# Turning the fourth tile of probabilities by DMA, scores in four banks, and a first head left unnormalized

## The chip, the core and the metric

The kernel runs on one core of one Trainium2 chip. A core has five engines that run their own instruction queues in order: TensorE (PE, with PEld for its weight loads), VectorE (DVE), ScalarE (ACT), GpSimd (POOL) and SyncE (SP), which here does nothing but issue DMAs. Matmuls write to PSUM, in banks of 128 partitions by 2 KB; the other tiles lie in SBUF. An engine waits for another through semaphores, and everything that stands behind a waiting instruction in the same queue waits with it.

The metric is the device time of one execution, in microseconds (us), as the median of several runs. Before the change it is 2786.77 us (three runs, 2785.22 to 2790.01 us).

## The reference

One block of a network: adaptive layer norm, attention over a window of cached keys and values, a second norm, and a gated MLP. Only the attention is touched by the change.

```python
W = min(4096, max(256, Sk // 4))          # 512 of 2048 cached positions
rep = Hq // Hkv                           # 32 query heads, 16 key heads
q = (x @ wq).reshape(B, Sq, Hq, Dh).transpose(0, 2, 1, 3)
k = jnp.repeat(k_cache[:, :, Sk - W:, :], rep, axis=1)
v = jnp.repeat(v_cache[:, :, Sk - W:, :], rep, axis=1)
scores = jnp.einsum("bhqd,bhkd->bhqk", q, k) * (Dh ** -0.5)
p = _softmax(scores, axis=-1)
o = jnp.einsum("bhqk,bhkd->bhqd", p, v)
return o.transpose(0, 2, 1, 3).reshape(B, Sq, Hq * Dh) @ wo
```

There are 2048 query rows of width 576, heads of 128, and an MLP of width 4608. Inputs and output are float32.

## The kernel before

Every float32 operand of a large matmul is split into two float16 tiles, a high part (the rounded value) and a low part (what is left). A product then takes three float16 matmuls: high by high, high by low, low by high.

**Slots.** The attention runs over 128 slots. A slot `i` is one query head on one block of 512 rows; the two heads that share a key head (`j` = 0 and 1) stand next to each other, so even slots are a first head and odd slots a second one. A slot has four steps, `t` = 0 to 3, one for each tile of 128 rows. The loop at the end of `tile_block` (L1465 to L1511) writes all queues by hand; the order of its calls is the order on each engine. Work of the MLP's preparation (splitting its weights, storing them) and the loading and splitting of the next heads' weights are hung in between by a table of tasks for each step (`run(i, t)`), and the last slots already begin the MLP.

**What happens to one tile.** `scores(i, t)` makes 128 by 512 scores with three matmuls in a PSUM bank (L400, from the pair of banks tagged "S"), and DVE takes their maximum (L404, L405, into one of three pairs of columns `nms`). `weights` takes the exponential on ACT (L417), which also sums the row into a column of `l`. The probabilities `p` must then be turned, because the value matmuls need the keys on the partitions. Tiles 0, 1 and 2 are split first, high by ACT (`half_high`, L449) and low by POOL (`half_low`, L454), into `hp`, and SP issues a DMA that turns both halves into `ptw` (`turn_away`, L461), two steps after the exponential's step. Tile 3 goes another way: at step 1 of the next slot PE turns the float32 tile with four transposes into a "T" bank (`turn`, L440), ACT copies the high part out of it (`turn_high`, L444), and at step 2 DVE subtracts for the low part (`turn_low`, L469).

**What happens to a slot.** At the end of slot `i`, after step 3, `values(i - 1)` runs its twelve matmuls of 512 columns (L479); each reads all four tiles of `ptw`. Queries of slot `i + 1` (L342, L346) are made in steps 0 to 2 of slot `i`, and each step holds one piece of the output projection of an older pair of heads (`back`, L353), two pieces of which fill the tile `E` (two banks, one buffer) that DVE then adds to `acc` (L507). The sums `l` are inverted on DVE (L424), stored as one row in DRAM (L427) and spread over all partitions as `r` by a second DMA (L430). At step 1 of slot `i + 2`, `normalize` multiplies the values by `r` on DVE (L488), and at step 3 `split_on` splits the result with ACT (L498) and POOL (L499) into the `o` that the projection reads.

**Buffers.** There are two "S" banks, two "T" banks, two "A" banks (queries and values take turns), four buffers of `p`, four of the tag `hf` (here `hp`), two of `ptw`.

## Time and profile before

| | before |
|---|---|
| median of three runs | 2786.77 us |
| lowest and highest | 2785.22 and 2790.01 us |
| the profiled execution | 2786.65 us |
| its span in the profile | 2784.8 us |
| granted TensorE clock | 0.996 |
| DMA packets, bytes | 594421, 463.27 MB |

The span runs from the first instruction of the program to the last; the profiled execution's own time is 1.85 us longer. "Busy" is the time in which an engine has an instruction in work; matmuls overlap, and their ends are modelled, so a PE that is shown busy can still have gaps. The chain in the page's fourth part is followed back from the last instruction to whatever released each step; PE has 50% of it, and the other engines and DMAs that it lists 6% together. In views that list a group, the numbers are its busy time in us, the mean duration of one instruction in ns, and behind the bar the idle time of the engine just before these instructions, with what ended it.

### The profile page before, as it was taken

How to read it: one execution, taken by the hardware profiler on the slowest of the kernel's cores; microseconds unless marked ns; L12 is line 12 of the kernel's file. 1: busy time of each engine (PE TensorE's matmuls, PEld its weight loads, DVE VectorE, ACT ScalarE, POOL GpSimd, SP SyncE). 2: the span in 40 equal slices, each digit the busy share in tenths (PEclk: the TensorE clock that was granted, in tenths of full speed). 3: DMA queues.
4: the chain of work that ended last, by engine and by line, in shares of the span. 5: the costliest groups of instructions: out<-in, count | busy, mean ns of one | idle time of the engine just before them, and what ended most of it. 6: DMA issues, size and time to landing. Idle time of an engine off the chain costs nothing.

```text
span 2784.8 us, 45011 instructions
## 1 busy us (share of the span) xinstructions
PE 2707.0 (97%) x15536; PEld 1535.3 (55%) x15536; DVE 2002.7 (72%) x3556; ACT 1624.1 (58%) x3022; POOL 1864.4 (67%) x1729
## 2 busy tenths in 40 slices
PE   6999999999999999999999999999999999999998
PEld 3455555555555555555555555555555555555555
DVE  7776788777788787887876657777766656566566
ACT  4686777777777877777677635544443333333332
POOL 3567788888788877777669637688774455333435
PEclk9999999999999999999999999999999999999999
DMA  5777888877777888878879945656643444333332
GB/s 162 177 168 187 189 186 185 179 178 187 169 181 172 187 200 186 212 181 205 194 185 220 233 125 169 195 165 199 206 152 103 160 123 127 104 102 112 105 110 77
DMA packets 594421, 463.27 MB, mean 166 GB/s; under 512 B 443152, under 2 KB 472976, under 8 KB 593424
## 3 DMA queue, kind: packets, MB, share of 16 engines
q1 hardware_dynamic: 593584, 460.39, 64.4%
q8 instruction: 122, 2.00, 0.3%
q14 instruction: 107, 0.88, 0.1%
q10 hardware_dynamic: 608, 0.00, 0.0%
HBM read 263.60 MB, written 95.99 MB: 129 GB/s over the span
## 4 chain that ended last, share of the span: by engine, by line
PE 50%; DVE 3%; DMA 1%; POOL 1%; issue 1%; ACT 0%; SPq 0%; DVEq 0%; POOLq 0%; ACTq 0%
PE py L764 15%; PE px L764 11%; PE pe L849 7%; PE pf L849 6%; PE pe L353 3%; PE po L479 2%; PE pss L400 2%; PE pq L342 2%; DMA row<-l 1%; DMA r<-row 0%; PE pt L440 0%; DVE acc L507 0%; DVE table L404 0%; PE pq L346 0%; POOL hp L454 0%
## 5 line engine op out<-in xcount | busy, mean ns | idle before, releaser
L454 POOL TENSOR_TENSOR hp<-p,hp 128x512 f16<-128x512 f32 x384 | 447.9, 1169 | 285.3 <-ACT hp L449 161.9
L417 ACT ACTIVATE p<-pss,table,factors 128x512 f32<-128x512 f32 x512 | 396.9, 775 | 362.0 <-DVE table L405 183.9
L764 PEld LDWEIGHTS <-wset 128*128 128x128 f16 x3528 | 345.7, 98 | 336.7 <-issue 4.0
L404 DVE TENSOR_REDUCE table<-pss 128x1 f32<-128x512 f32 x512 | 350.5, 685 | 211.8 <-PE pss L400 210.7
L764 PE MATMUL py<-hset,wset 128*128 128x512 f16 x2016 | 483.6, 380 | 0.0
L353 PE MATMUL pe<-o 128*128 128x288 f16 x3072 | 458.8, 286 | 14.6 <-DVE acc L507 12.5
L400 PE MATMUL pss<-k,qT 128*128 128x512 f16 x1536 | 417.3, 380 | 11.2 <-ACT p L417 9.2
L353 PEld LDWEIGHTS <-o 128*128 128x128 f16 x3072 | 300.4, 98 | 187.8 <-issue 20.9
L479 PE MATMUL po<-ptw,v 128*128 128x512 f16 x1536 | 358.2, 381 | 7.4 <-DVE ptw L469 5.6
L764 PE MATMUL px<-hset,wset 128*128 128x512 f16 x1512 | 361.5, 379 | 1.6 <-ACT p L417 1.6
L342 PE MATMUL pq<-hT,wq 128*128 128x512 f16 x1092 | 281.3, 380 | 1.1 <-DVE hT L211 1.1
L91 POOL TENSOR_TENSOR akv<-u,akv 128x512 f16<-128x512 f32 x141 | 164.8, 1178 | 174.6 <-ACT akv L90 166.8
L449 ACT CAST hp<-p 128x512 f16<-128x512 f32 x384 | 237.3, 618 | 12.9 <-POOL hT L213 0.4
L479 PEld LDWEIGHTS <-v 128*128 128x128 f16 x1536 | 150.9, 100 | 169.6 <-issue 16.8
L849 PEld LDWEIGHTS <-akv 128*128 128x128 f16 x1728 | 169.6, 98 | 93.6 <-issue 4.5
L400 PEld LDWEIGHTS <-qT 128*128 128x128 f16 x1536 | 150.4, 100 | 123.5 <-issue 12.6
L507 DVE SCALAR_TENSOR_TENSOR acc<-pe,factors,acc 128x576 f32<-128x576 f32 x256 | 207.7, 812 | 13.7 <-PE pe L353 10.4
L499 POOL TENSOR_TENSOR o<-on,o 128x512 f16<-128x512 f32 x128 | 150.2, 1173 | 55.8 <-ACT o L498 52.4
L342 PEld LDWEIGHTS <-wq 128*128 128x128 f16 x1104 | 108.6, 98 | 138.4 <-issue 9.0
L843 DVE SCALAR_TENSOR_TENSOR acc<-pf,table,acc 128x576 f32<-128x576 f32 x140 | 113.5, 811 | 80.6 <-PE pf L849 80.6
L944 ACT COPY u<-py 128x512 f32<-128x512 f32 x72 | 42.2, 586 | 200.5 <-PE py L764 198.6
L937 ACT ACTIVATE s<-s,table 128x512 f32<-128x512 f32 x72 | 52.0, 722 | 173.0 <-DVE s L936 173.0
(228 smaller groups left out, 4826.4 us busy)
## 6 DMA issues: line engine op xcount, KB each, us to landing
wset<-wd SPq DMA_DIRECT2D x213, 320.0 KB, 3.2
r<-row SPq DMA_DIRECT2D x128, 256.0 KB, 4.0
oset<-od SPq DMA_DIRECT2D x106, 288.0 KB, 3.2
wraw<-in_w SPq DMA_DIRECT2D x36, 768.0 KB, 5.5
wd<-wmade SPq DMA_DIRECT2D x75, 320.0 KB, 3.2
wset<-wd SPq DMA_DIRECT2D x71, 160.0 KB, 2.2
w2raw<-in_w SPq DMA_DIRECT2D x19, 576.0 KB, 4.9
wd<-ring SPq DMA_DIRECT2D x33, 320.0 KB, 2.8
```

What stands on the lines that cost most here:

```text
L91: eng.tensor_sub(halves[:, 1], src, halves[:, 0])
L342: nc.tensor.matmul(ps, w[:, k // 2, m, :], hT[:, DC + m if k == 1 else m, :], start=s == 0, stop=False)
L353: nc.tensor.matmul(E[:, h, :HALF], o[:, x, rows], w[:, y, h * HALF : (h + 1) * HALF], start=first and n == 0, stop=last and n == 2,)
L400: nc.tensor.matmul(pss, q[:, x, rows], k[:, y, :], start=n == 0, stop=n == 2)
L404: nc.vector.tensor_reduce(nm[:, 0:1], pss, axis=AX.X, op=ALU.max, negate=True)
L417: nc.scalar.activation(p, pss, AF.Exp, bias=nm[:, 1:2], scale=factor, accum_out=st["l"][:, t : t + 1])
L449: nc.scalar.copy(hp[:, 0, :], state[i]["p", t])
L454: nc.gpsimd.tensor_sub(hp[:, 1, :], state[i].pop(("p", t)), hp[:, 0, :])
L479: nc.tensor.matmul(po, v[:, x, c, :], pt[:, y, c, :], start=c == 0 and n == 0, stop=c == KC - 1 and n == 2)
L507: nc.vector.scalar_tensor_tensor(a, E[:, :, :HALF], factors[:, uses[u][0], 2:3], a, op0=ALU.mult, op1=ALU.add)
L764: nc.tensor.matmul(ps, w[:, a, :], h[:, b, :], start=start and n == 0, stop=stop and n == 6, skip_group_check=True)
L849: nc.tensor.matmul(ps[:, h, :HALF], a[:, rows], w[:, b, :], start=m == 0, stop=m == 2)
```

## The change

1. `turn`, `turn_high` and `turn_low` are gone. All four tiles go through `half_high`, `half_low` and `turn_away`. The fourth tile's `turn_away` stands at step 1 of the next slot, one step behind the third tile's.
2. Scores of tiles 0 and 2 go to the "T" banks that the transposes used, those of tiles 1 and 3 stay in "S".
3. The first head of a pair is no longer divided by its sums. `take_first` (ACT, step 0 of slot `i + 2`, one step before `normalize`) scales the values by 2^-24 straight from PSUM into the high part of `o`, and `normalize` makes the low part with one DVE instruction; its POOL subtraction, its row and its `r` are not made.
4. The second head is multiplied by the sum of the first over its own sum, so that both heads of a pair carry the same factor, one over the first head's sum. `E` is added to `acc` with that factor (a column of `l`) in place of a constant of the head. `l` is one tile for the pair, and DVE makes the ratio (a `scalar_tensor_tensor` on four columns) and the factor (a `tensor_scalar` on four columns) once a pair.

```diff
 def scores(i, t):
-        pss = bank("S", "pss")
+        pss = bank("S", "pss") if t % 2 else t_bank()
 def weights(i, t):
-            st["l"] = odd.tile([P, 2 * ST], F32, tag="l", name="l", bufs=3)
+            st["l"] = odd.tile([P, 6 * ST], F32, tag="l", name="l", bufs=4) if j == 0 else state[i - 1]["l"]
...
 def sums(i, step):
+        u, j, b = slots[i]
         st = state[i]
+        if j == 0:
+            return
+        first, both, up, ratio = (st["l"][:, lo * ST : hi * ST] for lo, hi in ((0, 1), (0, 2), (2, 4), (4, 5)))
         if step == 0:
-            nc.vector.reciprocal(st["l"][:, ST:], st["l"][:, :ST])
+            nc.vector.reciprocal(up, both)
+            nc.vector.scalar_tensor_tensor(ratio, first, O_DOWN, up[:, ST:], op0=ALU.mult, op1=ALU.mult)
         elif step == 1:
             st["row"] = dram.tile([P, ST], F32, name=f"row{i}")
-            nc.sync.dma_start(st["row"], st["l"][:, ST:])
+            nc.sync.dma_start(st["row"], ratio)
...
+    def take_first(i):
+        st = state[i]
+        o = st["o"] = new_o(i)
+        nc.scalar.activation(o[:, 0, :], st["po"], AF.Copy, scale=O_DOWN)
+
     def normalize(i):
         st = state[i]
         po = st.pop("po")
+        if slots[i][1] == 0:
+            o = st["o"]
+            nc.vector.scalar_tensor_tensor(o[:, 1, :], po, O_DOWN, o[:, 0, :], op0=ALU.mult, op1=ALU.subtract)
+            return
...
     def split_on(i):
         st = state[i]
+        if slots[i][1] == 0:
+            return
         on = st.pop("on")
-        o = st["o"] = pool.tile([P, 2, SB], F16, tag=("ah", "al")[i % 2], name="o", bufs=3)
+        nc.vector.tensor_scalar(
+            st["l"][:, 5 * ST :], st["l"][:, 2 * ST : 3 * ST], factors[:, uses[slots[i][0]][0], 2:3], 1.0 / O_DOWN,
+            op0=ALU.mult, op1=ALU.mult,
+        )
+        o = st["o"] = new_o(i)
...
 def attend_out(pair, t, j, total):
-                a, E[:, :, :HALF], factors[:, uses[u][0], 2:3], a, op0=ALU.mult, op1=ALU.add
+                a, E[:, :, :HALF], state[2 * pair]["l"][:, 5 * ST + t : 5 * ST + t + 1], a, op0=ALU.mult, op1=ALU.add
...
-            if t == 0 and 1 <= i <= n:
-                turn_away(i - 1, 2)
-            slot, tile = (i - 1 if t == 1 else n, ST - 1)
-            if 0 <= slot < n:
-                turn(slot, tile)
+            if t < 2 and 1 <= i <= n:
+                turn_away(i - 1, t + 2)
...
-            if 1 <= i <= n and t == 2:
-                turn_low(i - 1, ST - 1)
...
-            if t < 3 and i < n:
+            if i < n:
                 half_high(i, t)
                 half_low(i, t)
-            if t == 1 and 1 <= i <= n:
-                turn_high(i - 1, ST - 1)
+            if 2 <= i <= n + 1 and t == 0 and slots[i - 2][1] == 0:
+                take_first(i - 2)
```

How the queues move is shown at one place, slot 62 (a first head) and the beginning of slot 63. **SP**, from the first turning DMA of slot 62 on, before; `hp_9267`, `hp_9305` and `hp_9340` are its tiles 0 to 2, `hp_9407` is tile 0 of slot 63, `row61` and `row62` the sums of slots 61 and 62:

```order
L461 DMA_TRANSPOSE ptw_9329<-hp_9267 128x8x128
L636 DMA wd15_119<-wmade_9238 128x1280
L430 DMA r_9358<-row61_9309 128x512
L461 DMA_TRANSPOSE ptw_9329<-hp_9305 128x8x128
L461 DMA_TRANSPOSE ptw_9329<-hp_9340 128x8x128
L636 DMA wd15_119<-wmade_9323 128x640
L427 DMA row62_9447<-l_9264 128x4
L461 DMA_TRANSPOSE ptw_9464<-hp_9407 128x8x128
L636 DMA od70_168<-omade_9381 128x1152
L430 DMA r_9494<-row62_9447 128x512
```

The same place after; `hp_8901`, `hp_8937`, `hp_8970` and `hp_9000` are the four tiles of slot 62, `hp_9036` is tile 0 of slot 63:

```order
L455 DMA_TRANSPOSE ptw_8960<-hp_8901 128x8x128
L643 DMA wd15_119<-wmade_8872 128x1280
L436 DMA r_8988<-row61_8940 128x512
L455 DMA_TRANSPOSE ptw_8960<-hp_8937 128x8x128
L455 DMA_TRANSPOSE ptw_8960<-hp_8970 128x8x128
L643 DMA wd15_119<-wmade_8954 128x640
L455 DMA_TRANSPOSE ptw_8960<-hp_9000 128x8x128
L455 DMA_TRANSPOSE ptw_9085<-hp_9036 128x8x128
L643 DMA od70_168<-omade_9011 128x1152
```

The fourth tile's DMA has come in where the row of slot 62's sums stood, and that row and its `r` are gone.

**POOL**, from tile 0 of slot 62 to tile 0 of slot 63, before (`w2raw`, `wmade` and `omade` belong to the MLP's weights, `wq` to a later head):

```order
L454 TENSOR_TENSOR hp_9267<-p_9265,hp_9267 128x512
L275 TENSOR_TENSOR wq_9283<-wraw_8889,wq_9283 128x640
L735 TENSOR_TENSOR w2raw_8925<-w2raw_8925 128x288
L738 TENSOR_TENSOR w2raw_8925<-w2raw_8925 128x288
L454 TENSOR_TENSOR hp_9305<-p_9303,hp_9305 128x512
L686 TENSOR_TENSOR wmade_9323<-wraw_8707,wmade_9323 128x256
L687 TENSOR_TENSOR wmade_9323<-wraw_8707,wmade_9323 64x128
L454 TENSOR_TENSOR hp_9340<-p_9338,hp_9340 128x512
L499 TENSOR_TENSOR o_9370<-on_9301,o_9370 128x512
L718 TENSOR_TENSOR omade_9381<-w2raw_8925,omade_9381 128x2x288
L454 TENSOR_TENSOR hp_9407<-p_9405,hp_9407 128x512
```

And after:

```order
L448 TENSOR_TENSOR hp_8901<-p_8899,hp_8901 128x512
L276 TENSOR_TENSOR wq_8920<-wraw_8534,wq_8920 128x640
L742 TENSOR_TENSOR w2raw_8569<-w2raw_8569 128x288
L745 TENSOR_TENSOR w2raw_8569<-w2raw_8569 128x288
L448 TENSOR_TENSOR hp_8937<-p_8935,hp_8937 128x512
L693 TENSOR_TENSOR wmade_8954<-wraw_8368,wmade_8954 128x256
L694 TENSOR_TENSOR wmade_8954<-wraw_8368,wmade_8954 64x128
L448 TENSOR_TENSOR hp_8970<-p_8968,hp_8970 128x512
L448 TENSOR_TENSOR hp_9000<-p_8998,hp_9000 128x512
L725 TENSOR_TENSOR omade_9011<-w2raw_8569,omade_9011 128x2x288
L448 TENSOR_TENSOR hp_9036<-p_9034,hp_9036 128x512
```

In this even slot the low half of tile 3 takes the place of the subtraction of `o` (L499); in an odd slot both stand there.

**DVE**, steps 0 to 2 of slot 62 before (`table` holds the maxima):

```order
L404 TENSOR_REDUCE table<-pss 128x1
L405 TENSOR_SCALAR table<-table,factors 128x1
L424 RECIPROCAL l<-l 128x4
L404 TENSOR_REDUCE table<-pss 128x1
L405 TENSOR_SCALAR table<-table,factors 128x1
L488 TENSOR_TENSOR on<-po,r 128x512
L507 SCALAR_TENSOR_TENSOR acc_87<-pe,factors,acc_87 128x576
L404 TENSOR_REDUCE table<-pss 128x1
L405 TENSOR_SCALAR table<-table,factors 128x1
L469 TENSOR_TENSOR ptw<-pt,ptw 128x4x128
```

And after (`pt` is now a bank of scores):

```order
L405 TENSOR_REDUCE table<-pt 128x1
L406 TENSOR_SCALAR table<-table,factors 128x1
L429 RECIPROCAL l<-l 128x8
L430 SCALAR_TENSOR_TENSOR l<-l 128x4
L405 TENSOR_REDUCE table<-pss 128x1
L406 TENSOR_SCALAR table<-table,factors 128x1
L486 SCALAR_TENSOR_TENSOR o<-po,o 128x512
L514 SCALAR_TENSOR_TENSOR acc_87<-pe,l,acc_87 128x576
L405 TENSOR_REDUCE table<-pt 128x1
L406 TENSOR_SCALAR table<-table,factors 128x1
```

The subtraction from PSUM at step 2 (L469) is gone, the multiplication by `r` is another instruction in the first head's turn, and the small ratio has come in at step 0. Once a pair, at step 3 of the slot behind, the factor comes in as `L500 TENSOR_SCALAR l<-l,factors 128x4`.

18 lines of the change are left out of this document (4 added, 14 removed).

## The prediction

> **What bounds the kernel now.** I read the page's head first, then the busy time by stage (columns: stretch, its length, busy us of PE, PEld, DVE, ACT, POOL with counts, granted clock, mean share of the DMA engines, GB/s).
>
> ```profile
> span 2784.8 us, 45011 instructions
> PE 2707.0 (97%) x15536; PEld 1535.3 (55%) x15536; DVE 2002.7 (72%) x3556; ACT 1624.1 (58%) x3022; POOL 1864.4 (67%) x1729
> ```
>
> ```profile
> 260.00:1030.00 770.00, 759.05 (x4368) 429.18 (x4366) 608.22 (x1211) 595.77 (x1154) 652.75 (x630) 1.00 0.80 184
> 1030.00:1620.00 590.00, 577.31 (x3350) 329.30 (x3349) 435.51 (x878) 422.23 (x823) 419.95 (x386) 1.00 0.85 200
> 1620.00:2784.00 1164.00, 1148.21 (x6649) 651.77 (x6647) 763.68 (x1050) 428.80 (x718) 645.37 (x567) 1.00 0.43 137
> ```
>
> PE is busy over 97% of every stage, at a full clock. The change touches the attention, up to 1620 us; the MLP behind it stays. The reader should also see that POOL is busy 652.75 of 770 us (85%) in the first of these stretches and the DMA engines 80 to 85%: the side engines have little room, and the change gives both of them work.
>
> Whether PE is bound by its own work there is read from the timeline of one slot (62: its tile 3 is scored at 810.01, turned at 816.49, used at 823.01; start, duration, instructions, count):
>
> ```profile
> 810.01 0.81 PE L400 MATMUL pss<-k,qT 128*128 128x512 f16 x3 [0.34 <-ACT p L417]
> 810.65 0.90 PE L353 MATMUL pe<-o 128*128 128x288 f16 x6
> 811.39 2.80 PE L479 MATMUL po<-ptw,v 128*128 128x512 f16 x12
> 814.02 0.81 PE L400 MATMUL pss<-k,qT 128*128 128x512 f16 x3
> 814.67 1.24 PE L342 MATMUL pq<-hT,wq 128*128 128x512 f16 x5
> 815.75 0.90 PE L353 MATMUL pe<-o 128*128 128x288 f16 x6
> 816.49 0.60 PE L440 MATMUL pt<-ident,p 128*128 128x128 f32 x4
> 816.92 0.81 PE L400 MATMUL pss<-k,qT 128*128 128x512 f16 x3
> ...
> 823.01 2.32 PE L479 MATMUL po<-ptw,v 128*128 128x512 f16 x10
> ```
>
> From 811.39 on each group starts when the one ahead has issued its last matmul; the only bracket, the idle time, stands at 810.01. Over the whole run PE's waits in front of these groups are small (the last part of a row is idle us and what ended it):
>
> ```profile
> L353 PE MATMUL pe<-o 128*128 128x288 f16 x3072 | 458.8, 286 | 14.6 <-DVE acc L507 12.5 <-DVE us L251 1.8
> L400 PE MATMUL pss<-k,qT 128*128 128x512 f16 x1536 | 417.3, 380 | 11.2 <-ACT p L417 9.2 <-ACT qT L384 1.1 <-DVE qT L390 0.7
> L479 PE MATMUL po<-ptw,v 128*128 128x512 f16 x1536 | 358.2, 381 | 7.4 <-DVE ptw L469 5.6 <-DMA ptw<-hp 1.0 <-ACT ptw L444 0.3
> ```
>
> So **TensorE's instruction stream sets the time**, and the other engines only where they are late.
>
> **What goes from PE.** The four transposes of a slot hold PE from 816.49 to 816.92, 0.43 us. 128 slots give **-55 us**, the size of the change's gain if nothing else is late. Neighbours on PE keep their order, so nothing moves into the gap but what follows.
>
> **What is late next.** `values` needs all four tiles. For tiles 0 to 2 the DMA has long been the way, and it is nearly always in time (1.0 us of waits above). Tile 3 now takes the same way, its DMA one step behind tile 2's on SP. In slot 62, on ACT, POOL and PE:
>
> ```profile
> 813.94 0.77 ACT L417 ACTIVATE p<-pss,table,factors 128x512 f32<-128x512 f32 x1
> 814.60 0.20 ACT L417 ACTIVATION_READ_ACCUMULATOR p<-pss,table,factors 128x1 f32 x1
> ```
>
> ```profile
> 816.71 1.16 POOL L454 TENSOR_TENSOR hp<-p,hp 128x512 f16<-128x512 f32 x1
> 817.83 1.16 POOL L499 TENSOR_TENSOR o<-on,o 128x512 f16<-128x512 f32 x1
> ```
>
> ```profile
> DMA to landing us min/median/max: 3.0/3.8/8.2
> ```
>
> The exponential of tile 3 ends at 814.71, the high copy (0.62 us) could end at 815.4, but POOL subtracts tile 2 until 817.87; the new subtraction follows in the place of L499, to 819.0. With the median landing of 3.8 us the tile is there at 822.8; PE, 0.43 us earlier than before, wants it at 822.6. PE waits 0.2 us. This slot is about the middle: I took for every slot the time from the end of tile 3's exponential to the first value matmul, and took from it the time that tile 2 of the same slot needed from its exponential to its landing, and 0.43. The ends of the 128 slots:
>
> ```profile
> 50.45 0.79 ACT L417 ACTIVATE p<-pss,table,factors 128x512 f32<-128x512 f32 x1
> ```
>
> ```profile
> 66.38 1.87 PE L479 MATMUL po<-ptw,v 128*128 128x512 f16 x4
> ```
>
> ```profile
> 1602.51 0.79 ACT L417 ACTIVATE p<-pss,table,factors 128x512 f32<-128x512 f32 x1
> ```
>
> ```profile
> 1619.58 2.75 PE L479 MATMUL po<-ptw,v 128*128 128x512 f16 x12
> ```
>
> These two have 15.1 and 16.3 us, far enough; but the median is 9.6 us, and 42 slots of 128 come out late, by 51 us in sum. A wait in one slot gives the next slot's tile the same time, because its scores were issued ahead of the waiting matmuls; counted so, slot after slot, the sum is 40 us. With tile 0's time to landing, the quickest, it is 12 us; if the tile is 1 us later still than tile 2's, it is 71 us. Two things pull at this. POOL gets 128 more subtractions and loses 64, while DVE and ACT lose work just ahead of tile 3:
>
> ```profile
> L454 POOL TENSOR_TENSOR hp<-p,hp 128x512 f16<-128x512 f32 x384 | 447.9, 1169 | 285.3 <-ACT hp L449 161.9 <-issue 79.3 <-DVE table L405 16.8
> L499 POOL TENSOR_TENSOR o<-on,o 128x512 f16<-128x512 f32 x128 | 150.2, 1173 | 55.8 <-ACT o L498 52.4 <-PE pss L400 1.2 <-POOL wmade L687 0.7
> L469 DVE TENSOR_TENSOR ptw<-pt,ptw 128x512 f16<-128x512 f32 x128 | 87.6, 684 | 26.6 <-ACT ptw L444 25.5 <-DMA row<-l 0.4 <-issue 0.2
> L444 ACT CAST ptw<-pt 128x512 f16<-128x512 f32 x128 | 74.1, 579 | 0.6 <-PE pt L440 0.6
> ```
>
> POOL: 128 x 1.169 - 64 x 1.173 = +75 us, 0.58 us a slot. A slot lasts (1619.58 - 66.38)/127 = 12.2 us; 85% of it is 10.4 us, so POOL would want 11.0 of 11.8 us, 93%. That lengthens its queue; the 0.68 us of DVE at step 2, just ahead of tile 3's maximum, shortens the way to the exponential. I let these two cancel and take **+40 us**, bounds 12 and 71.
>
> **What else moves.** Waits that go: those for `ptw` on DVE and ACT (5.6 + 0.3) with their instructions, and the 9.2 us for a bank of scores, since PE now has four and runs two tiles further ahead before it needs an exponential's bank. The 12.5 us for `acc` I leave, since DVE's load hardly falls (below). **-15 us**, bounds 0 and -28 (all three rows' named waits).
>
> DVE loses 128 x 0.684 = 88 us. In the first head's turn it makes the low half as the queries' row does, 0.690 for 1.085 us, 64 times, -25 us:
>
> ```profile
> L488 DVE TENSOR_TENSOR on<-po,r 128x512 f32<-128x512 f32 x128 | 138.9, 1085 | 16.8 <-POOL o L499 8.4 <-DMA r<-row 6.1 <-PE po L479 1.8
> L390 DVE SCALAR_TENSOR_TENSOR qT<-pq,qT 128x512 f16<-128x512 f32 x127 | 87.6, 690 | 63.5 <-ACT qT L384 63.0
> L233 DVE TENSOR_SCALAR us<-us 128x4 f32<-128x4 f32 x15 | 11.3, 752 | 0.5
> L233 DVE TENSOR_SCALAR us<-us 128x1 f32<-128x1 f32 x19 | 2.9, 154 | 0.7
> ```
>
> It gains two instructions on 128x4 a pair, 128 in all, between 0.154 and 0.752 us each: 20 to 96 us. The last two rows are the same line on four columns and on one; the longer mean is not work. The ratio has two SBUF operands, so I take the upper row, 96 us, and DVE nets -17 us: no relief counted, and no cost, since it is off the path at 77%. The Trainium skill (SBUF — State Buffer, "SBUF: two separate sides") says that GpSimd and VectorE share a pair of ports under an exclusive lock, which a VectorE instruction with two SBUF inputs or in a two-port mode waits for; the two rows agree with that, and by it the small instructions would cost up to one POOL instruction each, which still stays off the path.
>
> ACT: 128 copies of 618 in place of 579 ns, +5 us, hidden at 75% busy. The first head's high part is read from PSUM one step earlier by ACT; DVE's low half stands behind it in the queue and can wait for ACT, and `acc` (L507) and the next maxima stand behind that. This replaces the wait for `r` (6.1 us above) in half of the slots; I put it at nothing, bounds -6 and +6. A buffer of `hp` now comes round after 4 tiles, not 5 1/3: ACT's copy of tile k+4 needs the DMA that SP issues at step k+2 to have landed, two steps (some 5.8 us) for a median of 3.8. ACT will wait sometimes; its 25% of idle time hides that. SP gains 1.24 us of issue a slot and loses two short ones every second slot. The DMA engines gain a third more turning DMAs and lose half of the 256 KB spreads; at 0.81 to 0.85 I expect somewhat later landings, which is within the bounds of the 40.
>
> **Sum**, against the profiled execution's own 2786.65 us (1.85 beyond its span, and 0.1 from the median): 2786.65 - 55 + 40 - 15 = **2757 us**.
>
> **The rivals.**
>
> *The tile is in time.* If DVE's shorter queue brings tile 3's exponential forward and it lands as quickly as tile 0 does, the wait is 12: 2786.65 - 55 + 12 - 15 = 2729 us. For it: PE's own 1.0 us of waits on these DMAs. Against it: that row is of a tile with one step more time.
>
> *The last tile becomes the bound (slower).* Its place is the first value matmul of each slot; its price is the wait there; it decides from 70 us in sum, 0.55 us a slot, where it eats the 55 and the 15. That is reached when tile 3 lands 1 us later than the count above assumes. The mechanism is POOL at 93%: its queue runs behind (in slot 62 it already subtracts tile 2 four us after the high copy), SP issues two DMAs back to back, and each lands later (8.2 at most). 1.4 us later gives 88 us, and with none of the 15 saved 2820 us; with them, 2805. Against it: a waiting PE gives POOL time, so the queue can't grow for long. The Trainium skill (VectorE: DVE Perf Modes, "Rules for kernel authors", with the figures of "The three transpose paths") speaks against the change too: 128x128 blocks are to be transposed on TensorE where PSUM will do as the destination, and by DMA otherwise, with 390 ns against 1309 ns for one. The trace agrees that a DMA takes longer (3.8 us to landing against 0.60 for the four on PE), but the 3.8 us lie beside PE's work unless the tile is late.
>
> *It evens out.* The wait is 65 to 75: 2781 to 2792, no difference.
>
> **How the numbers follow.** Chances: forecast (2740 to 2781) 0.52; tile in time (2720 to 2740) 0.18; evens out 0.10; slower 0.20. The likeliest is 2757. To hold 8 in 10 the range takes the forecast, the first rival, the no-change case and the lower part of the slower one: 2722 to 2800. Faster by more than 0.2% (5.6 us, about what a measurement of this kernel can tell from no change): 0.70; within: 0.10; slower: 0.20.
>
> **What would show it.** Right: no L440 rows; some 40 us of idle time in front of the value matmuls, ended by the DMA of `ptw`, in a third of the slots; under 3 us in front of scores for ACT; POOL busy 90% or more up to 1030 us; the four-column instructions of DVE near 0.75 us. Wrong: the waits at the value matmuls under 15 us (then the first rival) or over 70; PE waiting for `acc` by much more than 12.5 us (then DVE's new wait for ACT, which I put at nothing); or a slot as long as before with PE idle elsewhere.

## The result and the profile after

| | before | after |
|---|---|---|
| median of four runs each, side by side | 2786.91 us (2785.22 to 2790.01) | 2820.94 us (2817.19 to 2824.32) |
| ratio, with its 95% interval | | 1.0124 (1.0111 to 1.0137) |
| the profiled execution | 2786.65 us | 2823.43 us |
| its span | 2784.8 us | 2821.6 us |
| granted TensorE clock | 0.996 | 0.987 |

The changed kernel is slower by 34 us. The prediction was 2757 us, with a range that ended at 2800: the sign is wrong, and the time lies beyond the range.

The head of the page after, with each engine's busy time and instructions:

```profile
span 2821.6 us, 44006 instructions
PE 2678.1 (95%) x15024; PEld 1480.2 (52%) x15024; DVE 1971.4 (70%) x3492; ACT 1637.1 (58%) x3022; POOL 1935.5 (69%) x1793
```

PE has its 512 transposes less and 29 us less busy time, but it is busy 95% and no longer 97%. The busy time by stage, after (the same columns as before: stretch, its length, busy us of PE, PEld, DVE, ACT and POOL, granted clock, share of the DMA engines, GB/s):

```profile
260.00:1030.00 770.00, 731.92 (x4037) 395.40 (x4036) 583.42 (x1159) 592.08 (x1134) 674.70 (x649) 0.98 0.84 188
1030.00:1620.00 590.00, 551.17 (x3077) 299.56 (x3075) 421.58 (x855) 427.40 (x829) 455.99 (x421) 0.99 0.92 206
1660.00:2821.00 1161.00, 1145.24 (x6637) 649.59 (x6634) 762.87 (x1050) 428.56 (x718) 645.12 (x567) 1.00 0.43 137
```

The loss lies in the attention: of 770 us PE now misses 38 where it missed 11, and in the second stretch 39 of 590 where it missed 13. The MLP behind it is as before. The groups of PE, after (busy us, mean ns, and behind the bar idle us ahead of them with what ended it):

```profile
L354 PE MATMUL pe<-o 128*128 128x288 f16 x3072 | 464.2, 288 | 30.4 <-DVE acc L514 23.6
L468 PE MATMUL po<-ptw,v 128*128 128x512 f16 x1536 | 369.1, 392 | 61.0 <-DMA ptw<-hp 45.7
L401 PE MATMUL pt<-k,qT 128*128 128x512 f16 x768 | 210.9, 382 | 6.9 <-ACT qT L385 3.2
L401 PE MATMUL pss<-k,qT 128*128 128x512 f16 x768 | 212.2, 386 | 0.0
```

PE's idle time ahead of the value matmuls went from 7.4 to 61.0 us and ahead of the projection (`back`) from 14.6 to 30.4. The value matmuls also became longer: 1536 of them take 369.1 us in place of 358.2.

**One late tile.** Four views of one stretch after: PE, POOL, SP's issues and the granted clock. First PE (start, duration):

```profile
741.72 2.54 PE L468 MATMUL po<-ptw,v 128*128 128x512 f16 x11
...
751.27 0.81 PE L401 MATMUL pss<-k,qT 128*128 128x512 f16 x3
751.91 1.10 PE L354 MATMUL pe<-o 128*128 128x288 f16 x6
755.67 4.14 PE L468 MATMUL po<-ptw,v 128*128 128x512 f16 x12 [2.65 <-DMA ptw<-hp]
```

The matmuls at 755.67 use the tile 3 whose high copy on ACT is this row:

```profile
743.12 0.62 ACT L443 CAST hp<-p 128x512 f16<-128x512 f32 x1
```

POOL's queue behind that copy:

```profile
743.74 1.61 POOL L693 TENSOR_TENSOR wmade<-wraw,wmade 128x512 f16<-128x512 f32 x1
745.42 0.67 POOL L694 TENSOR_TENSOR wmade<-wraw,wmade 64x256 f16<-64x256 f32 x1
746.17 1.41 POOL L737 TENSOR_TENSOR w2raw<-w2raw,gate_b 128x576 f32<-128x576 f32 x1
747.53 1.16 POOL L448 TENSOR_TENSOR hp<-p,hp 128x512 f16<-128x512 f32 x1
748.64 0.79 POOL L739 TENSOR_TENSOR w2raw<-w2raw 128x288 f32<-128x288 f32 x1
749.52 0.80 POOL L740 TENSOR_TENSOR w2raw<-w2raw 128x288 f32<-128x288 f32 x1
750.27 1.16 POOL L448 TENSOR_TENSOR hp<-p,hp 128x512 f16<-128x512 f32 x1
```

And SP's issue of its DMA:

```profile
751.46 1.24 SPq L455 DMA_TRANSPOSE ptw<-hp  x1
```

The copy is done at 743.74, but POOL works through five pieces of the MLP's weights and tile 2's low half (747.53) first and ends tile 3's at 751.43, 7.7 us later. SP issues at once, the DMA lands 4.2 us behind, and PE has waited 2.65 us. Of the 12.5 us from the start of the copy to the matmul, POOL's queue made 6.5.

The twelve matmuls then take 4.14 us, where eleven had taken 2.54 at 741.72. The busy time of three pieces of this stretch shows why; the last three columns are the granted clock, the DMA engines' share and GB/s:

```profile
755.67:757.00 1.33, 1.33 (x6) 0.60 (x7) 1.33 (x2) 1.30 (x4) 1.33 (x2) 0.96 0.00 0
757.00:758.40 1.40, 1.40 (x5) 0.52 (x4) 0.39 (x1) 0.41 (x1) 1.40 (x2) 0.50 0.58 114
758.40:759.40 1.00, 1.00 (x4) 0.36 (x3) 0.00 (x0) 0.00 (x0) 1.00 (x2) 0.50 1.03 266
```

Behind the wait the clock falls to half: the last six of the twelve matmuls start 0.43 us apart, where 0.22 us is usual. So this wait is paid twice.

**The account of PE's stream.** For each run I added up the spacing between the starts of successive matmuls, from 100 us to the last matmul of the projection. Spacing at full speed (216 ns behind a matmul of 512 columns, 122 behind one of 288, 109 behind a float32 transpose) is work; what exceeds it is a gap ahead of a group, or slowness inside a group; us:

| kernel | work | gap ahead of scores | of the projection | of the values | of others | inside groups | at half clock |
|---|---|---|---|---|---|---|---|
| before | 1494.6 | 8.5 | 13.4 | 1.8 | 4.2 | 17.0 | 0 |
| after | 1436.6 | 5.5 | 32.2 | 65.1 | 5.6 | 31.6 | 51.2 |

The differences are -58.0 + (-3.0 + 18.8 + 63.3 + 1.4) + 14.6 = +37 us, which is the difference of the spans (36.8). The columns of gaps and of slowness are those used for the experiments below.

### The profile page after: what moved, and what is told of

Same layout as the page of the kernel before. It is cut to its first block, busy times and chain, and to the rows that moved or that the text cites. A ratio compares the mean times of both kernels' runs of the same rounds, so it can differ in the third digit from the quotient of the medians.

```text
span 2821.6 us, 44006 instructions
## 1 busy us (share of the span) xinstructions
PE 2678.1 (95%) x15024; PEld 1480.2 (52%) x15024; DVE 1971.4 (70%) x3492; ACT 1637.1 (58%) x3022; POOL 1935.5 (69%) x1793
## 5 line engine op out<-in xcount | busy, mean ns | idle before, releaser
L448 POOL TENSOR_TENSOR hp<-p,hp 128x512 f16<-128x512 f32 x512 | 595.0, 1166 | 292.0 <-ACT hp L443 159.0
L354 PE MATMUL pe<-o 128*128 128x288 f16 x3072 | 464.2, 288 | 30.4 <-DVE acc L514 23.6
L468 PE MATMUL po<-ptw,v 128*128 128x512 f16 x1536 | 369.1, 392 | 61.0 <-DMA ptw<-hp 45.7
L418 ACT ACTIVATE p<-pt,table,factors 128x512 f32<-128x512 f32 x256 | 198.3, 775 | 324.0 <-DVE table L406 286.4
L443 ACT CAST hp<-p 128x512 f16<-128x512 f32 x512 | 316.4, 618 | 35.7 <-DMA ptw<-hp 18.8
L405 DVE TENSOR_REDUCE table<-pss 128x1 f32<-128x512 f32 x256 | 176.1, 688 | 154.6 <-PE pss L401 154.4
L405 DVE TENSOR_REDUCE table<-pt 128x1 f32<-128x512 f32 x256 | 174.4, 681 | 90.5 <-PE pt L401 90.1
L418 ACT ACTIVATE p<-pss,table,factors 128x512 f32<-128x512 f32 x256 | 197.9, 773 | 35.9 <-DVE table L406 33.3
L514 DVE SCALAR_TENSOR_TENSOR acc<-pe,l,acc 128x576 f32<-128x576 f32 x256 | 207.5, 811 | 15.5 <-PE pe L354 12.9
L401 PE MATMUL pt<-k,qT 128*128 128x512 f16 x768 | 210.9, 382 | 6.9 <-ACT qT L385 3.2
L401 PEld LDWEIGHTS <-qT 128*128 128x128 f16 x1536 | 151.0, 100 | 126.5 <-DVE qT L391 8.1
L401 PE MATMUL pss<-k,qT 128*128 128x512 f16 x768 | 212.2, 386 | 0.0
```

The lines of the kernel that those rows point to most:

```text
L354: nc.tensor.matmul(E[:, h, :HALF], o[:, x, rows], w[:, y, h * HALF : (h + 1) * HALF], start=first and n == 0, stop=last and n == 2,)
L401: nc.tensor.matmul(pss, q[:, x, rows], k[:, y, :], start=n == 0, stop=n == 2)
L405: nc.vector.tensor_reduce(nm[:, 0:1], pss, axis=AX.X, op=ALU.max, negate=True)
L418: nc.scalar.activation(p, pss, AF.Exp, bias=nm[:, 1:2], scale=factor, accum_out=st["l"][:, j * ST + t : j * ST + t + 1])
L443: nc.scalar.copy(hp[:, 0, :], state[i]["p", t])
L448: nc.gpsimd.tensor_sub(hp[:, 1, :], state[i].pop(("p", t)), hp[:, 0, :])
```

## The experiments

All times are medians beside the kernel before on the same chip, ratios with their 95% intervals.

| kernel | us | ratio to before |
|---|---|---|
| tiles_only | 2860.76 | 1.0272 (1.0257 to 1.0287) |
| first_only | 2784.73 | 0.9998 (0.9989 to 1.0007) |
| late_low | 2815.20 | 1.0108 (1.0091 to 1.0125) |
| values_later | 2920.28 | 1.0490 (1.0469 to 1.0511) |
| early_first | 2818.34 | 1.0107 (1.0092 to 1.0122) |
| dve_low | 2831.74 | 1.0159 (1.0143 to 1.0174) |
| halves | 2810.72 | 1.0079 (1.0064 to 1.0094) |
| all_three | 2802.75 | 1.0048 (1.0031 to 1.0065) |
| scores_early | 2816.66 | 1.0107 (1.0092 to 1.0123) |
| scores_early_first | 2816.35 | 1.0099 (1.0083 to 1.0116) |
| scores_early_halves | 2801.47 | 1.0051 (1.0036 to 1.0066) |
| old_tile3 | 2797.75 | 1.0038 (1.0025 to 1.0051) |
| before_pool | 2807.49 | 1.0072 (1.0057 to 1.0087) |
| before_hf3 | 2792.94 | 1.0021 (1.0012 to 1.0031) |
| old_tile3_early | 2783.26 | 0.9984 (0.9975 to 0.9994) |
| even_only | 2803.84 | 1.0058 (1.0041 to 1.0074) |
| no_o | 2803.41 | 1.0058 (1.0039 to 1.0076) |
| old_tile3_no_o | 2763.56 | 0.9912 (0.9894 to 0.9929) |

### Which part costs: the tiles or the first head

**tiles_only** is the kernel before with parts 1 and 2 of the change: four tiles by DMA, scores in four banks, both heads divided by their sums as before.

```diff
...
-            slot, tile = (i - 1 if t == 1 else n, ST - 1)
-            if 0 <= slot < n:
-                turn(slot, tile)
+            if t < 2 and 1 <= i <= n:
+                turn_away(i - 1, t + 2)
...
```

> The first part of the change alone: all four tiles split and turned by DMA, scores in four banks; both heads are normalized as before. Theory (the last tile lands after PE wants it): the 55 us of transposes go, the waits in front of the value matmuls are 70 to 90 us (POOL here has 75 us more to do than in the whole change, as the first head keeps its subtraction), PE's wait for DVE's addition to acc stays near the 13 us of before, and the time is 2810 to 2830 us. Rival (the loss is made by the first head's new path on ACT and DVE): the waits at the values stay under 40 us and the time is 2755 to 2775 us.

**first_only** is the kernel before with parts 3 and 4: tile 3 on PE, two banks of scores, the first head unnormalized.

```diff
...
+            if 2 <= i <= n + 1 and t == 0 and slots[i - 2][1] == 0:
+                take_first(i - 2)
...
```

> The second part alone: the first head unnormalized and read early, the second times the ratio; the fourth tile is turned by PE as before and scores have two banks. Theory: DVE's low half waits for ACT's high half in even slots, the addition to acc stands behind it, and PE waits 25 to 40 us for acc in the even slots' step 2; nothing else changes much: 2795 to 2815 us. Rival (the new path is harmless, DVE and POOL only gain): 2770 to 2787 us, PE's wait for acc 13 us or less.

Measured: the tiles alone cost 75 us, the first head alone nothing (-1 us, within the interval), both together 34. Both theories missed: tiles_only lies beyond its 2810 to 2830 us, above all because the wait for `acc`, expected near 13 us, was 41.5; first_only came out as its rival had it. The projection's row in tiles_only:

```profile
L353 PE MATMUL pe<-o 128*128 128x288 f16 x3072 | 462.9, 288 | 50.2 <-DVE acc L507 41.5
```

and in first_only:

```profile
L354 PE MATMUL pe<-o 128*128 128x288 f16 x3072 | 459.0, 286 | 15.2 <-DVE acc L531 10.9
```

So the longer waits for `acc` come with the tiles, not with the first head by itself. DVE's new wait for ACT is in first_only too, nearly as long as the 21.0 us of the changed kernel, and costs PE next to nothing there. In tiles_only DVE waits for POOL's `o` instead (8.4 us before). One row of each; behind the colon stand the us in total, the times and the longest:

```profile
DVE o L503 <- ACT o L496: 19.4, 30, 1.0
DVE on L488 <- POOL o L499: 29.8, 17, 3.6
```

The first head's part, which saves POOL 64 subtractions and SP half of the rows and spreads `r`, is worth nothing alone and 40 us beside the tiles; which of its savings does that was not tried apart.

### Giving tile 3 more time

**values_later** makes the value matmuls one step later, behind step 0 of the next slot, and `take_first` and the first head's low half one step later too.

```diff
...
-        if 1 <= i <= n:
+            if 2 <= i <= n and t == 0:
+                values(i - 2)
+        if i == n:
             values(i - 1)
```

> The changed kernel with the value matmuls of a slot one step later (behind step 0 of the slot after next, not at the end of the next), and with them the reading of the first head (step 1) and the multiplication or low half on DVE (step 2, behind the addition to acc). Theory (the last tile only needs more time): waits at the values under 10 us, for acc under 10 us, granted clock back to 0.995: 2715 to 2740 us. Rival (POOL can't do its work in the shorter slot, so that the lateness only moves): POOL's lag grows until the waits come back, 2780 us or more.

The gap at the values falls to 0.6 us, and the kernel becomes slower still by 99 us. Its scores, in the view of groups:

```profile
L401 PE MATMUL pt<-k,qT 128*128 128x512 f16 x768 | 234.8, 389 | 159.5 <-ACT qT L385 126.2
```

The value matmuls at a slot's end (eleven of them take 2.54 us above) had been the cover under which ACT and DVE make the two halves of the next slot's `qT`. Without them there, PE waits for `qT` at the first scores of nearly every slot (120 times). The theory's waits were cured and its 2715 to 2740 us missed all the same; the rival had a slower kernel, but by POOL's lag, which did not bring the waits at the values back.

**scores_early** moves the scores of tile 3 to step 2, behind those of tile 2. **scores_early_first** and **scores_early_halves** add early_first and then halves, which stand below.

```diff
-            if i < n:
+            if i < n and t < 3:
                 scores(i, t)
+            if i < n and t == 2:
+                scores(i, 3)
```

> The changed kernel with the scores of tile 3 moved from step 3 to step 2, right behind those of tile 2 (the four banks allow it): tile 3's scores are ready one group of PE work earlier, about 1.6 us. Theory (the last tile is late by the length of its own route; in the changed kernel the waits at the values that exceed 1.6 us sum to about 25 us): waits at the value matmuls fall from 65 to 20 to 35 us, time 2775 to 2800. Rival (POOL's queue sets the landing, and an earlier exponential only waits longer in front of POOL): waits at the values 50 us or more, time 2812 to 2825.

> scores_early and take_first ahead of the exponential of step 0 on ACT. Theory (two separate waits, one for tile 3 and one for acc behind DVE's wait for ACT): the waits for acc fall by about 10 us against scores_early, and the time by 5 to 12 us, to 2765 to 2792. Rival (curing one wait makes the other): as scores_early within 3 us.

> scores_early_first and the value matmuls in two halves of 256 columns, tiles 0 and 1 first, so that tile 3 has 1.3 us more before it is needed. Theory: waits at the values 5 to 15 us, but the 24 short matmuls cost PE about 24 us more inside the group as they did before (inside-group loss 71 us in the kernel with halves alone); time 2755 to 2790. Rival (the halves' own cost eats the gain): slower than scores_early_first by 5 us or more.

The gap at the values is 70.1 us in scores_early: no better. The theory of 20 to 35 us fell. Scores that are ready sooner don't bring the tile forward: from their end to the start of the exponential it now took 4.53 us on the mean in place of 2.56, and from there to the landing as long as in the changed kernel (9.3 us), because the exponential and what follows keep their places in ACT's and POOL's queues. The projection's gap falls to 17.0 and 9.0 us in the first two, those of the scores rise to 11.5 and 14.2; scores_early_halves gains 19 us, about what all_three below does without this move. The rivals of the first two held; scores_early_halves missed both its theory (2755 to 2790 us) and its rival, which had it slower than scores_early_first.

**halves** makes the values in two halves of 256 columns, tiles 0 and 1 first.

```diff
+        for half in range(2):
+            cols = slice(half * SB // 2, (half + 1) * SB // 2)
...
-                    po, v[:, x, c, :], pt[:, y, c, :], start=c == 0 and n == 0, stop=c == KC - 1 and n == 2
+                        po[:, cols], v[:, x, c, :], pt[:, y, c, cols],
```

> The changed kernel with the value matmuls in two halves of columns: first those of tiles 0 and 1, then those of tiles 2 and 3, 24 matmuls of 256 columns in place of 12 of 512, so that tile 3 has 1.3 us more. Theory (arrival): of the 68 us that PE waits there, what is above 1.3 us in each wait remains, 27 us, the granted clock falls less often, and the time is 2770 to 2795 us, if 256 columns cost half of 512. Rival (PE's waits only move, because POOL or DVE can't keep the shorter slot): 2805 us or more.

**dve_low** makes tile 3's low half on DVE at the head of the next slot's step 0 and not on POOL.

```diff
+            if t == 0 and 1 <= i <= n:
+                half_low(i - 1, 3, nc.vector)
...
                 half_high(i, t)
-                half_low(i, t)
+                if t < 3:
+                    half_low(i, t)
...
```

> The changed kernel with the fourth tile's low half made by DVE at the head of the next slot's step 0, not by POOL: POOL gets 150 us less, DVE 128 subtractions from SBUF of some 1.1 us more. Theory (the last tile is late because POOL's queue runs behind): from the end of ACT's copy to the end of the low half 2.9 us on average falls to 2 us or less, without the late ones of 5 to 11 us, and the gaps ahead of the value matmuls fall from 65 to 20 to 35 us: 2775 to 2805 us, less the more DVE's waits for acc grow. Rival (the way through DVE, ACT and DMA is too long for a tile with one step less, whoever subtracts): the gaps stay above 50 us.

**early_first** puts `take_first` ahead of the exponential of step 0 on ACT.

```diff
+            if 2 <= i <= n + 1 and t == 0 and slots[i - 2][1] == 0:
+                take_first(i - 2)
             if i < n:
                 weights(i, t)
...
-            if 2 <= i <= n + 1 and t == 0 and slots[i - 2][1] == 0:
-                take_first(i - 2)
```

> The changed kernel with ACT's high half of the first head ahead of the exponential of step 0, not behind its copy. Theory (PE's wait for acc at step 2 of even slots comes from DVE's low half standing behind that ACT instruction): the gaps ahead of the projection's matmuls fall from 32 to under 15 us, those ahead of the value matmuls stay at 55 to 75 us: 2795 to 2810 us. Rival (DVE's order or its load at step 1 is the cause, whatever ACT does): the gaps stay above 25 us and the time within 5 us of 2821.

**late_low** puts the first head's low half on DVE a step later, behind `acc`.

```diff
-            if 2 <= i <= n and t == 1:
+            if 2 <= i <= n and t == 1 + (i % 2 == 0):
                 normalize(i - 2)
```

> The changed kernel with the first head's low half on DVE one step later (step 2, behind the addition to acc). Theory: PE's 29 us of waits for acc at step 2 of even slots fall under 8 us, the waits at the value matmuls stay at 60 to 80 us: 2793 to 2806 us. Rival (DVE is late for another reason, or the wait only moves to step 3 and the maxima): 2813 us or more.

> The three together: early high half of the first head, fourth low half on DVE, values in two halves. Theory: gaps ahead of the values under 15 us, ahead of the projection under 20 us, little low clock: 2730 to 2760 us, faster than before. Rival (another engine sets the slot's length once the tile is in time): 2780 us or more.

All_three is early_first, dve_low and halves together. Halves gains 10 us, all_three 18, late_low 6, early_first 3, and dve_low loses 11. By the account each cures its own wait and feeds another: dve_low brings the gap at the values from 65.1 to 38.2 us and the projection's from 32.2 to 66.4, since `acc` stands behind the new instruction on DVE; late_low brings the projection's from 32.2 to 10.8 and the scores' from 5.5 to 15.8; halves has nothing left ahead of its groups of values, but 39 us of waits in their middle. In time, halves, all_three, late_low and early_first came out as their rivals had it (early_first's gap ahead of the projection, 21.9 us, lies between its theory's 15 and its rival's 25); dve_low's 38.2 us lies between its theory's 35 and its rival's 50, and its time above the theory's 2805. No version of this kind comes near the kernel before.

### Taking the arrival away

**old_tile3** lets the DMA of a slot's tile 3 write into the `ptw` of the next slot. Queues and loads stay; only the arrival of the last tile can no longer be late.

```diff
+        if t == ST - 1 and 1 < i < n - 1:
+            state[i + 1]["pt"] = pool.tile([P, 2, KC, SB], F16, tag="pt", name="ptw")
+            to = [2, 3] if i == 2 else [i + 1]
...
```

> The changed kernel, but the DMA of a slot's tile 3 writes into the ptw of the slot behind it, so that the value matmuls read tile 3 of the slot before and never wait for a DMA of the last step; engines, DMAs and the order of all queues are as in the changed kernel (slot 2 has one DMA more). It leaves out the right probabilities of tile 3. Theory (the late fourth tile is the cause: 63 us of waits at the value matmuls, and the low granted clock behind them): waits there under 5 us, granted clock 0.995 or more, waits for acc near the 32 us of the changed kernel, time 2740 to 2765, faster than before. Rival A (the waits only move, as when the values were put one step later: PE then waits for qT, acc or a bank of scores instead): waits elsewhere grow by 40 us or more, time 2790 or more. Rival B (the DMA engines' and POOL's load itself slows the attention): time 2780 to 2815 with PE's instructions themselves longer.

Its two rows:

```profile
L354 PE MATMUL pe<-o 128*128 128x288 f16 x3072 | 464.6, 288 | 49.3 <-DVE acc L519 33.7
L473 PE MATMUL po<-ptw,v 128*128 128x512 f16 x1536 | 360.1, 385 | 14.4 <-DMA ptw<-hp 10.5
```

The idle time at the values falls from 61.0 to 14.4 us, but the time by 23 us only. The projection's rises from 30.4 to 49.3. So 2740 to 2765 was wrong, and the time is rival A's, though the other gaps grew by 28 us and not by its 40 (the table below). It lies in rival B's range too, but B's sign is weak: the value matmuls take 385 ns, 381 before and 392 in the changed kernel. With the arrival cured, gaps and slowness are still 85.9 + 29.6 us against 27.9 + 17.0 before. What makes these 71 us was tried one resource at a time.

**before_pool** gives the kernel before 75 us more on POOL, by making an even slot's `o` low half twice; **before_hf3** gives it three buffers of `hf`.

```diff
-        nc.gpsimd.tensor_sub(o[:, 1, :], on, o[:, 0, :])
+        for _ in range(2 - i % 2):
+            nc.gpsimd.tensor_sub(o[:, 1, :], on, o[:, 0, :])
...
-HF, STORE = 4, 3
+HF, STORE = 3, 3
```

> The kernel before, with POOL's low half of o made twice in every even slot: 64 x 1.17 = 75 us more on POOL, at the step where the change puts tile 3's low half, and nothing else. Theory (a, POOL's load makes acc late): time 2800 to 2830, waits for acc 30 us or more. Rival (b or c): 2785 to 2795, waits for acc under 18 us.

> The kernel before, with three hf buffers in place of four: a buffer comes round after one slot, as in the changed kernel. Theory (b, ACT's wait for the turning DMAs delays what stands behind it): ACT waits 20 to 50 us for DMAs of ptw, waits for acc 25 us or more, time 2800 to 2820. Rival: ACT's idle time hides it, 2785 to 2793.

**old_tile3_early** is old_tile3 with early_first.

> old_tile3 with take_first ahead of the exponential of step 0 on ACT; tile 3's probabilities are again those of the slot before. Theory (c, DVE's low half waits for ACT): gaps in front of the projection fall from 51 to 25 us or less, time 2765 to 2785. Rival (a or b, ACT and POOL are late as a whole): gaps 40 us or more, 2790 to 2800.

**even_only** turns only the even slots' tile 3 by DMA; odd slots use PE.

```diff
+            if t == 1 and 1 <= i <= n and i % 2:
+                turn_away(i - 1, 3)
+            if t == 1 and 1 <= i <= n and i % 2 == 0:
+                turn(i - 1, ST - 1)
...
```

> The changed kernel, but only even slots turn their tile 3 by DMA; odd slots do it on PE as before (64 x 0.43 = 27 us of transposes stay), so POOL has as many instructions in every slot as the kernel before. Theory (a, POOL's queue sets the landings and acc): waits at the values under 20 us, for acc under 18 us, time 2760 to 2782, faster than both. Rival (the last tile's route is too long whatever POOL does): waits at the values about 29 us, those of the even slots now, and the clock's loss with them: 2785 to 2805.

**no_o** is the changed kernel without POOL's low half of the second head's `o`; **old_tile3_no_o** is old_tile3_early without it.

```diff
         nc.scalar.copy(o[:, 0, :], on)
-        nc.gpsimd.tensor_sub(o[:, 1, :], on, o[:, 0, :])
...
```

> The changed kernel without POOL's low half of the second head's o (which it leaves out; the projection reads the high part in its place): POOL has as much work as in the kernel before, tile 3 still comes by DMA. Theory (the route's own length makes tile 3 late): gaps at the values 45 to 65 us, time 2795 to 2812, slower than before. Rival (POOL's added work made the tile late, as the prediction's slower rival had it): gaps at the values under 35 us, time 2785 or less.

> old_tile3_early without POOL's low half of the second head's o, 64 x 1.17 = 75 us: POOL has as much work as in the kernel before. It leaves out that low part (the projection reads the high part in its place) and the right probabilities of tile 3. Theory (POOL's added work makes the remaining waits): gaps in front of the projection and at the values together under 20 us (41 in old_tile3_early), time 2745 to 2765. Rival (they come from elsewhere, the buffers of hp or the DMA engines): 2775 or more.

The account for these runs, us:

| kernel | work | gap ahead of scores | of the projection | of the values | of others | inside groups | at half clock |
|---|---|---|---|---|---|---|---|
| before_pool | 1492.9 | 7.8 | 22.2 | 6.5 | 4.2 | 28.1 | 13.7 |
| before_hf3 | 1491.9 | 9.5 | 13.8 | 3.9 | 7.0 | 19.9 | 3.4 |
| old_tile3 | 1436.8 | 7.6 | 51.4 | 14.5 | 12.4 | 29.6 | 34.1 |
| old_tile3_early | 1436.0 | 9.6 | 29.0 | 12.0 | 10.8 | 37.0 | 23.9 |
| even_only | 1467.1 | 18.9 | 15.3 | 30.5 | 6.0 | 21.3 | 20.5 |
| no_o | 1438.4 | 7.8 | 26.1 | 56.4 | 6.8 | 25.0 | 34.1 |
| old_tile3_no_o | 1439.1 | 8.7 | 20.5 | 21.1 | 8.8 | 20.3 | 20.5 |

Measured against what was expected: no_o came out as its theory had it, even_only as its rival, each in gap and time. old_tile3_early and before_pool have their theory's time, but 29.0 us ahead of the projection where 25 was the bound, and 22.2 us for `acc` where 30 was. before_hf3 has its rival's time. old_tile3_no_o has its theory's time but not its reason: the two gaps together stay at 41.6 us (41.0 without the edit), and the gain lies mainly inside groups (37.0 to 20.3).

What follows:

- **POOL's added work goes with some 20 us wherever it is put or taken away.** It adds 19 to 20 us to the kernel before (before_pool), and leaving 75 us out gains 18 in the changed kernel (no_o) and 20 in the one without the arrival wait (old_tile3_no_o against old_tile3_early). In before_pool the multiplication by `r` on DVE waits for POOL, two thirds of it in the first head's turn, and `acc` stands behind it:

```profile
DVE on L488 <- POOL o L500: 20.8, 13, 3.1
PE pe L353 <- DVE acc L508: 22.2, 21, 2.6
```

  Before, these were 8.4 and 12.5 us. These edits change what has to wait for POOL's `o` together with POOL's load, and the two were not tried apart. In old_tile3_early PE itself waits for `o`, a wait that old_tile3_no_o leaves out:

```profile
PE pe L354 <- POOL o L511: 11.0, 6, 2.3
```

- **Most of the arrival wait is not made by that added work.** With POOL's busy time as before (no_o: 648.93 us from 260 to 1030 us, before 652.75), PE still waits for the tiles; the gap falls from 65.1 to 56.4 us:

```profile
L468 PE MATMUL po<-ptw,v 128*128 128x512 f16 x1536 | 367.6, 391 | 53.2 <-DMA ptw<-hp 42.2
```

  In even_only, also with POOL as before, 64 tiles by DMA have a gap of 30.5 us, (30.5 - 1.8)/64 = 0.45 us a tile; in the changed kernel it is (65.1 - 1.8)/128 = 0.49. A transposing group on PE had cost 58.0/128 = 0.45. The route through ACT, POOL, SP and a DMA, one step shorter than tile 2's, gives back on the average just what it saves.
- **`take_first` late on ACT** is worth 14 us once the arrival wait is gone (old_tile3_early against old_tile3: the projection's gap falls from 51.4 to 29.0), and 3 us while it is there.
- **The buffers of `hp`** cost 4 to 6 us by themselves (before_hf3). ACT's wait there is 18.8 us, as in the changed kernel:

```profile
ACT hp L449 <- DMA ptw<-hp: 18.8, 16, 3.1
```

- With arrival, `take_first` and POOL's load all cured, the kernel is 22 us faster than before. That shows where the expected gain went, up to 21 us of gaps that remain at the values. Their trace shows them to be tile 2's: in 14 of the 15 slots with a gap of more than 0.2 us its DMA landed last, 0.04 to 0.25 us ahead of the first matmul. In nine of these POOL ended tile 2's low half 4.4 to 8.2 us after the copy (1.2 at least), in five SP issued its DMA 2.6 to 8.2 us after the low half. Of the versions that can be used, none beats the kernel before by more than can be measured.

## Why the prediction was wrong, step by step

**Transposes, -55 us: right.** The work in PE's stream fell by 58.0 us, and PE stayed the engine whose stream sets the time.

**The last tile's wait, +40 us: the right place and mechanism, the size was off.** The gap grew by 63 us, and 37 of 128 slots had more than 0.2 us of it, each with tile 3 the last to land, 0.04 to 0.25 us ahead of the first matmul; I had counted 42 slots and 51 us before letting one slot's wait help the next. The first rival, 12 us, fell. The view of the line's waits has it in 40 places (27 of the matmuls, 13 of their weight loads):

```profile
  DMA ptw<-hp: 70.2, 40
```

The count took the time that tile 2 needed in the kernel before for tile 3. Tile 3 needs longer: from the end of the exponential to the landing it took 8.5 us on the mean after, tile 2 before 7.9. Most of that is POOL's: from the end of the high copy to the end of the low half tile 2 took 2.4 us before, tile 3 took 2.9 after (4.4 in the 37 late slots, 2.3 in the others, 1.23 at least). The prediction's slower rival, that the last tile becomes the bound, had the place and nearly the price (it was to decide from 70 us in sum), but the cause in part only: it put the wait down to POOL at 93%. POOL was at 674.70 of 770 us, 88%, and no_o and even_only show most of the wait with POOL's load of before. POOL's queue counts all the same: in 26 of the 37 late slots the low half ended more than 3 us after the copy, and dve_low, which takes tile 3 off POOL, brings the gap to 38.2 us.

**Waits that go, -15 us: this term failed, and with it the step that left PE's wait for `acc` as it was.** The gaps other than those at the values were to fall by 15 us and grew by 17 (-3.0 + 18.8 + 1.4). The waits for a bank of scores did go (9.2 us for ACT before; no such entry stands in the rows of L401 after), as did those for `ptw` on DVE; but the gap ahead of scores fell by 3.0 us only, some of it being for `qT` now (3.2 us, before 1.1). I left the wait for `acc` at its 12.5 us, "since DVE's load hardly falls", and put the new wait on ACT at nothing, bounds -6 to +6. It was the wait that grew: the gap ahead of the projection by 18.8 us. After, DVE's wait for ACT and PE's for `acc`:

```profile
DVE o L486 <- ACT o L479: 21.0, 31, 1.0
PE pe L354 <- DVE acc L514: 23.6, 22, 2.7
```

Of the projection's gap of 32.2 us, 29.3 stand at step 2 of the even slots, against 7.0 there before: just where `acc` stands behind the first head's low half on DVE. Moving `take_first` forward (early_first) brings those to 16.5, and the time down by 3 us only. DVE's wait for ACT is not the whole cause: first_only has 19.4 us of it and hardly more idle time ahead of the projection than before (15.2 against 14.6), and tiles_only has no such instruction and 50.2 us of that idle time. What the step had wrong is that it priced `acc` by DVE's load alone: DVE's busy time fell (2002.7 to 1971.4 us) and the wait grew, with the tiles. The prediction named this wait as what would prove it wrong; it did not price it, although what waits behind it (`acc`, then PE) was in its text.

**POOL's added work, priced at nothing on its own, goes with some 20 us.** I set it only against tile 3's landing and let it cancel with DVE's relief. before_pool shows that it acts without any tile: through `o`, DVE and `acc`. These 20 us are no further term; they lie within the gaps and the slowness counted here.

**The granted clock was not in the sum.** The slowness inside groups grew by 14.6 us. Counted from the same spacing, some 20 of its 31.6 us lie in the stretches at half clock, and some 10 outside of them, less than the 17 before. The Trainium skill (TensorE: Matmul & The Clock Gate, "Part 1: The HAM clock gate") says that TensorE's clock is gated to half when it has been idle for about a window of 3.4 us. The trace agrees with the half (0.50) and with the window, since each low stretch lasts 3.41 us or twice that; but here PE waits of 2.0 to 2.9 us brought it on in nine of thirteen cases.

**What was costed at nothing and was nothing:** the first head's part by itself (first_only, 0.9998). DVE's four-column instructions were put at 96 us; their two rows sum to 66, off the path:

```profile
L430 DVE SCALAR_TENSOR_TENSOR l<-l 128x4 f32<-128x4 f32 x64 | 35.8, 559 | 2.2
L500 DVE TENSOR_SCALAR l<-l,factors 128x4 f32<-128x4 f32 x64 | 29.9, 467 | 0.0
```

**The DMA's own length was not the trouble.** All turning DMAs together land no later than before, where the median was 3.8 us:

```profile
DMA to landing us min/median/max: 3.0/3.6/10.2
```

Those of tile 3 alone have a median of 3.4 us. What counts is the wait behind POOL and SP that a tile goes through first. The rule of the Trainium skill on transposes (VectorE: DVE Perf Modes, "Rules for kernel authors"), which speaks for TensorE, came out right here, though not by that length.

**Still open** is what keeps `acc` late when `take_first` is early (16.5 us at step 2 of the even slots, 7.0 before), and how much of the 20 us that go with POOL's work is its load and how much the waits for `o` itself; neither was tried apart.

## What to carry to other kernels

Work moved from a saturated engine to others saves its length only if the whole route, with each queue that it passes, ends before the cover does; price that route by its own queue places, not by a neighbour's that had a step more time. A kernel whose side engines are busy 75 to 88% can have a price for load that is "off the path": add the same load alone to the old kernel and measure it (here 75 us on POOL came with 20). And where a wait is cured by moving work, look first at what the moved work had been covering.

## What the runs showed of the hardware

- Short idle times can cost PE more than their length. In the changed kernel, between 100 us and the end of the projection, the granted clock was 0.50 in 13 stretches of 3.41 or 6.83 us, 51 us in all. Nine came with idle times of PE of 2.0 to 2.9 us, four with longer ones up to 5.5. It is no fixed length: four other idle times of 2.0 to 2.3 us brought no such stretch, nor did one of 2.9 us in the kernel before, which has none there.
- A DVE instruction on 128 by 4 elements took anything from 161 to 1166 ns (median 520), and another of the kind 218 to 1201, as the view of these lines has it:

```profile
L430 DVE SCALAR_TENSOR_TENSOR l<-l x64: 161/520/1166, 71.4 to 1639.3; 128x4 f32<-128x4 f32 x64
L500 DVE TENSOR_SCALAR l<-l,factors x64: 218/300/1201, 94.7 to 1660.6; 128x4 f32<-128x4 f32 x64
```
